# A third staging buffer for the spectrum, with a new written-out order: SSM convolution mixed with linear attention on one core

## The chip, the cores and the metric

The kernel runs on one core of one Trainium2 chip. The time is the device time of one execution in microseconds; the kernel before takes 255.44 us (median of three runs, 254.7 to 255.97). A core has TensorE (PE; its weight loads are shown as PEld), VectorE (DVE), ScalarE (ACT), GpSimd (POOL) and SyncE (SP), which here issues nearly all DMAs from one queue, in order. Each engine runs its own instructions strictly in the order in which they were written.

## The reference

Input x is [1, 2048, 512]; two branches are computed from it and mixed by a gate.

```python
x = A_u
g = sigmoid((x * gate_w).sum(-1, keepdims=True))
# branch a: a long convolution by FFT, its kernel K from a diagonal state space
dt = exp(log_dt)[:, None]
P = exp((dt * (A_re + 1j * A_im))[:, :, None] * l)          # 512 x 128 x 2048
K = einsum("dn,dnl,dn->dl", Cc, P, dt * Bc).real
a = irfft(rfft(pad(u)) * rfft(pad(K)))[:2048] + u * Dskip
# branch b: linear attention, 32 heads of 16, feature map of two softmaxes
phi(z) = concat(softmax(z @ w_phi), softmax(-(z @ w_phi)))
kv = einsum("bhsf,bhsd->bhfd", phi_k, v);  z = phi_k.sum(s)
o = (phi_q @ kv) / (phi_q @ z + 1e-6)
b = o @ wo
return g * a + (1 - g) * b
```

## The kernel before

The kernel is a graph of about 1040 nodes, each a few instructions of one engine or one DMA. Functions add nodes with their dependencies; then `Plan.run` writes them all out in one fixed order. Nothing is scheduled at run time: the string `ORDER` gives the sequence of nodes (two characters a node), `SIDES` says for each node that may run on either of two engines which one it takes (PSUM evictions, mostly, on ACT or DVE), `RINGS` says for each product that may use either of two groups of PSUM buffers which one, and `FOURS` and `ZPS` choose between two ways of doing a step. `Plan`'s first argument holds the number of buffers of each SBUF tile that rotates, among them `xst`.

In time the work runs like this.

- **Start (to about 29 us).** SP issues the loads: x transposed (`xT`, L498, in two halves of four), the value weights `WW`, the parameters of the state space, small weights, the transposed query and key weights, and x once more as `UD` in 16 DMAs (L1491). ACT makes sine tables (`TB`, `TI`, `TJ`); PE makes the first values `vp` (L678) and turns the parameters (`psri`); DVE scales them (L342 to L382); A and its high and low halves go through DRAM (`pz`, L349) into `statE` and `statC` (L358). PE folds w_phi into the weights (`wps`, L517), evicted to `WW` and `Wqp`. POOL builds index patterns, masks and `Wphi`; `selE` (L458) and `diagD` (L481) are made on DVE.
- **Keys and the spectrum of x (29 to 67 us).** For eight pairs of row blocks PE makes key products `pk`, ACT their exponentials `Ek` (both signs), PE or DVE the sums (`Zk`; `ZPS` says whether PE adds groups of four first), ACT the reciprocals (by logarithm and exponential), DVE the weighted values `vr`, and PE adds them into `kvp`. In between, the first half of the channels goes through the first FFT stages: `UDp` (copies of `UD`), PE `psA`, eviction to `XAu`, PE `psB` (L587), eviction to the staging tile `xst`, which two DMAs (L599) write to the DRAM tensor `XUd`. One `xst` tile takes two evictions (8 of 32 rows), 4 KB in each partition; there are eight such tiles, four for each half of the channels, in two buffers.
- **Tables and second half (67 to 99 us).** ACT loads the sine set; ACT and DVE in turn make the tables `Ctab` and `Dtab`. The second half of the channels goes through the same `XAu` and `xst` steps.
- **Main part (99 to 229 us).** For 16 units of 32 channels: ACT makes `E` and `cs`, DVE the factors `A` and `R` by products (L1098, L1103, L1115, L1119) and, where `FOURS` is 0, an add of two halves (L1108), PE the convolution kernel `kps` (L182; twice the matmuls where `FOURS` is 1). It is evicted (`KD`), transformed (`psA` to `XA`, `psB` to `XK`), multiplied on DVE by x's spectrum, read back from `XUd` into `XUX` (L1182, L1184), giving `t` (L1229); PE transforms back (`psz`), the result goes as `Zr` to DRAM (`Zd`, L1274) and returns turned as `ZT` (L1284); PE adds the attention output (`psy`), and DVE scales by the gate (L1362 to L1368) into `xT`. The queries (`pq`, `Eq`, `zs`, `ops`, `oT`) of four row blocks run in between; their normalisation goes through DRAM (`apd`, L897, and `ax`, L904). `ax` and `ZT` share one buffer. ACT changes between the exponential and the sine set ten times in all.
- **End (229 to 255 us).** The last 64 channels: units 12 and 13 as one group, 14 and 15 each alone (unit 15 is never written to DRAM: `pszn`, `Z`, L1353). The attention output of the fourth query block is made (`bps`, L944), scaled (`bsg`, L979 and L981, with `bs3`) and stored (L993); finished channels are stored (L1379).

`Plan` counts eight DMAs in flight (`ln`), and an issue takes one of these places.

The lines in question:

```python
X.s = g.kwk.tile([128, 4, 8, 64], BF16, name="xst", tag="xst", bufs=g.nxst)
...
P = Plan(nc, {"XAu": 1, "UDp": 1, "xst": 2, ...
g.P, g.PHASES, g.nxst = P, {0: 4, 4: 8, 8: 12, 12: 16}, P.k["xst"]
...
n.at = n.eng if isinstance(n.eng, str) else n.eng[int(next(sides, 0))]
...
for i in order:
    n = self.nodes[i]
    self.cur = n
    n.fn()
```

Of the kernel before, what the change touches and what calls it, by code (L numbers as in the profile page):

```python
# [70 lines left out]
class Plan:  # L71

    DIGITS = "0123456789abcdefghijklmnopqrstuvwxyzABCDEFGHIJKLMNOPQRSTUVWXYZ-_"
    ORDER = ("2B2C2D0H2H2K0L0K2I0E002E2L070y0d2J0j2M0I0J0M0S0N0W0P2v0T0Q0g0O010a0U0Y04050B2W0X110R0V2Q0Z0k02192w0F1612140_0h0z0G0i102T"
             "0b15171d1a0l1b2N2U0e2R2F2G4N0A2X2Y0-"
             "4L4M4O0c2O0f2x1H2V1e2S0306081w1c1f2P1n1o1p1g1q1r1s091x0m4P1y1I1z1B1Q1A1E1J0p0q0r1Y4Q1R1C2y0C0D2Z312-"
             "2_1F303334324C1D4J4K1G0n4V4X544W4Y5556571K4D4Z4-"
             "4_501S52581T0s4R1Z594E512z531U1V4F4S5a5b0t5f5h4T5c5d5e130v0w5g4U0o0u0x1O5i181N1W351P365q375s1M5j38395k3b5r5t5u5l3c3a3d3e"
             "3f5m5n5o5p5v3h3g3i5w5z5x5B5C3j3k3l3m4G5D1h1i5E5F5y5A1t3n3o5M5O1j5N5P5G3p3q3r5H3s5Q3w5I5J3x3y3z5K3t3A5R5S5L3R1L5X3D5Y5Z5-"
             "3B3E3S3T5_3U5V3F5T5U3G605W6a6c6b6d613K3L3M6e3N6f6g1X1_3u1-3V3W3X3Y3Z3-"  # L80
             "3C3_211k41203v27221l4042622363294344452b282d243H46642a2c252A4748492f2h3I2e2o3O3P4a4b1u4c2j4g4d2g2i4h262k2l2m2q4i4j664n2p"
             "2s4e4p4q4k4u2n654o2r4w4x6h6i1m3Q2t1v674v6j2u89686l8b8d4B6m8k694r4s4l8f8l888c8a6n6u8e4t3J8g6k6o6q4H8m6p4I8h8i8j4f8n8o6w6x"
             "6y6v8q8r8s6z6A6B4y8E8w4z8x8F718p8t8u4A8v7A7B4m6t6C6D6E8K7273748N6r6F6G8G8y8O7577956H8z8A8H8C768_6I8I8L787C8D6J8B797a6s7D"
             "a2a36K908J7E7F8P6L8T8U7b6M8M7c916P6Q6R8Qabac7G7H7d8R8S967e7f7g6N6Oad9U9Y9Z8V8Wa46T9V8X7h6Sa8a992936V6W9-6Ua5a6a78Y8Z8-"
             "ah9Xa06X9W6Zaiaa9_7i7j7k7la19b9c7I7Jaeaf9j7m7K7q9k7rap6Y9d7n7L7Maq7o6-"
             "7N949lagaj7O7P7Q7s7pakayaz7R7tar7Savaw977T9e9f9m9n7ubV7vbWaA9r9sbLbPasat7w7x9z7y9AbQalbM7V7W9tau7Uam7ZaEanbRao7_7z9g7X9h"
             "7-ax80aPbNaF6_98aS7YaBbS9o818370aT84aCbObTbU9982aDaG9ubX859v9a9pb_aH9B9C869DaMaN87c29wbYaUaQ9EbZc39x9yc0b-"
             "c4aIcpdMc8c99FcqaO9qaJaKaLc1cgdNdOc5chaYaZcraRc6cvcwb4a-"
             "cib5b6c7cabcdPbda_becbbkblcjezb79i9G9H9KaVb0b8dQdRcmckdScneA9Ib1bfbgaW9NdTdUcc9JaXcdeIcD9Ob2cl9Pb9dVcebmbhcfcM9L9McoeJcs"
             "cEbidWdCdGcteKdHeB9Q9R9SeFdDcudIcxcGeGeCeDcy9TbabnczcHcIdXdYcAdZcFcBcCe1dFeOcPd-"  # L90
             "d_eEe0bobpcQcRbqcXcYeHePbrb3e2cJcSdKcKe3e4bjdEbbeLeMcTe5cNbseNdJbycZbtcUcLd3e6dLdbd4dcd5eQeRc-"
             "cOe7e8cVc_bvfofpd6frddbwfqeScWd0bxenbueTfueUeVbzbAfsdebBd7dfeqd8eWfteXd1d2fvf2f3eoepbCd9dabDfRfSeYdgdhfwfxeZe-"
             "erdpbEdiesf4fUfVewf5f6djdkdldqexfXfyfWdmfzdndodseydte_f7f0etbFfTf8fYfZf-f_fAdudvg0eufBdrf1e9evg1g2g3fCfDfEeaebf9g4g6fafb"
             "fcfdbIedecfFfGg5feeeg7g8efegfffgg9dwehfhgagbgcgdfHfIfJfKfLfMgegffNfOdzekflfidAdBfmbJbKfnfjdxdyelembGbHeiejfPfQggghgjfkgi"
             "gkgl")
    SIDES = ("010100100000100011001000011000001110000000000010001011100111000000110010000000000000000000000000000000100000000000100001"
             "00001100100100000000100010001001101")
    RINGS = ("10111010000000000000000000000110000000000001000110000100000010111011111011100101011000001110000101010100000100110")
    WARM = ("000000000000000000000000000000000000000000000000000000000000000000000000000000000000000000000000000000000000000000000000"
            "000000000")  # L100
    FOURS = ("0101110101011010")
    ZPS = ("01110101")

    HOT = ("pk", "vp", "pq", "zp", "ops", "bps4", "psA", "psBu", "psB128", "psB64", "psB32", "psz", "pszn", "psyn32", "psy128", "psy64", "psy32", "kps")

# [46 lines left out]
    def run(self):  # L152
        code = {d: i for i, d in enumerate(self.DIGITS)}
        order = [64 * code[a] + code[b] for a, b in zip(self.ORDER[0::2], self.ORDER[1::2])] or list(range(len(self.nodes)))
        assert sorted(order) == list(range(len(self.nodes)))
        sides, rings, warm = iter(self.SIDES), iter(self.RINGS), iter(self.WARM)
        for n in self.nodes:
# [39 lines left out]

def prepare(P, nc, g, evict, psum):

# [431 lines left out]
def attention_keys(P, nc, g, psum, r):  # L631
# [57 lines left out]
    for s2 in range(8):  # L689
# [20 lines left out]

        def ps4(K=K, box=box, on=P.ZPS[s2] == "1"):
            if not on:
# [345 lines left out]
def plan_conv(P, nc, g, psum, r):  # L1058
# [27 lines left out]
    def kgen(units, XA, new, split=False):  # L1086
        K = Bag()
        K.done, kps, nu = [], [], len(units)
        for cc, U in enumerate(units):
            t = T[U]  # L1090
            plan_exp(P, nc, g, psum, U, t, psq, [sh])
            four = P.FOURS[U] == "1"
            c = Bag()
# [330 lines left out]
def full_kernel(tc, A_u, A_A_re, A_A_im, A_B_re, A_B_im, A_C_re, A_C_im, A_log_dt, A_Dskip,  # L1424
                B_x, B_wqkv, B_w_phi, B_wo, gate_w, out):
    nc = tc.nc
# [4 lines left out]
        return ctx.enter_context(tc.tile_pool(name=name, bufs=bufs, reuse_waits="tile", **kw))  # L1431
    with ExitStack() as ctx:
        g, fc, at = Bag(), Bag(), Bag()
        P = Plan(nc, {"XAu": 1, "UDp": 1, "xst": 2, "Ek": 2, "Zk": 2, "vr": 2, "vb": 2, "acc": 1, "r8": 3, "ax": 1, "nrm": 1, "E": 2, "cs": 4, "A": 1, "R": 2,
                      "KD": 1, "XA0": 1, "XK": 2, "Zr": 2, "XUX": 3, "ln": 8}, {"ps": 2, "p0": 2, "bk": 3, "acc": 1, "pf": 2})
        g.P, g.PHASES, g.nxst = P, {0: 4, 4: 8, 8: 12, 12: 16}, P.k["xst"]
        g.LAST = (((12, 13), True), ((14,), True), ((15,), False))
# [187 lines left out]
```

## Time and profile before

| what | value |
|---|---|
| median of three runs | 255.44 us |
| profiled execution: its own time | 256.34 us |
| profiled execution: span of the profile | 254.6 us |
| busy DVE / ACT / PE | 225.0 / 212.5 / 198.4 us |
| mean granted clock of TensorE | 0.952 |
| DMA moved | 38.03 MB, mean 149 GB/s |
| chain that ended last, shares | ACT 39%, DVE 21%, PE 15%, DMA 13%, issue 7% |

The page gives busy time by engine over the span, the span in 40 slices with the busy share in tenths, the groups of instructions by line and tile with their count and mean duration, and for each group the idle time before it with what ended it. Busy time by stretch, waits by pair, the timeline of one engine and the chain can be asked of the trace. "SPq" is SyncE's sequencer issuing a DMA: its time covers the wait before the issue only in part, and several issues of one line stand in one row with the time from the first's start to the last's end. The time of a PE row is modelled and includes the drain of its last matmul.

### The profile page before, as it was taken

To read this page: it belongs to the slowest core of one execution; us is meant where nothing else is said; L and a number is where in the kernel's file an instruction comes from. 1 tells how busy PE (TensorE), PEld (TensorE's weight loads), DVE (VectorE), ACT (ScalarE), POOL (GpSimd) and SP (SyncE) were. 2 spreads that over 40 slices of the span, in tenths; PEclk is the share of its full clock that TensorE was granted. 3 is DMA by queue.
4 is the path that set the end of the run, shared out by engine and by line. 5 is a ranking of instruction groups with operands and counts; after the bars stand their busy time and mean duration, and the time that the engine had idled before them with its cause. 6 is when DMAs were issued, how large, how long until landed. Compare 5 with 4: busy or idle time off the path is not lost.

```text
span 254.6 us, 9988 instructions
## 1 busy us (share of the span) xinstructions
PE 198.4 (78%) x4466; PEld 136.2 (53%) x4488; DVE 225.0 (88%) x308; ACT 212.5 (83%) x293; POOL 7.0 (3%) x19
## 2 busy tenths in 40 slices
PE   0295999999545769998668868998997799999940
PEld 0043466665435523565447556656775586777630
DVE  6769678897999998999999999999999999998631
ACT  4956799999899999999999999999897999744300
POOL 6040000000000000000000000000000000000000
PEclk9999999999995797999799999999999999999995
DMA  5999994009640869004340176155575397899666
GB/s 105 181 186 201 204 203 106 2 10 257 153 123 3 237 163 339 13 13 143 111 152 28 42 235 234 49 178 113 170 226 189 117 244 198 251 237 220 159 75 102
DMA packets 79755, 38.03 MB, mean 149 GB/s; under 512 B 58720, under 2 KB 74720, under 8 KB 79712
## 3 DMA queue, kind: packets, MB, share of 16 engines
q1 hardware_dynamic: 77312, 36.93, 56.3%
q8 instruction: 35, 0.57, 1.0%
q10 hardware_dynamic: 2400, 0.46, 1.0%
q14 instruction: 8, 0.07, 0.1%
HBM read 21.12 MB, written 13.11 MB: 134 GB/s over the span
## 4 chain that ended last, share of the span: by engine, by line
ACT 39%; DVE 21%; PE 15%; DMA 13%; issue 7%; SPq 4%; ACTq 0%; DVEq 0%
ACT cs L68 7%; ACT Ek L68 4%; DMA Zd<-Zr 3%; DMA XUd<-xst 3%; DMA ZT<-Zd 3%; PE kps L182 3%; ACT trg L68 3%; ACT Zr L148 3%; DVE R L1115 3%; ACT L65 3%; DVE R L1119 2%; DMA xT<-in_A_u_dram 2%; ACT XAu L148 2%; PE vp L678 2%; DVE A L1098 2%
## 5 line engine op out<-in xcount | busy, mean ns | idle before, releaser
L182 PE MATMUL kps<-R,A 128*32 128x64 bf16 x1600 | 29.6, 230 | 3.8 <-DVE A L1103 1.7
L182 PEld LDWEIGHTS <-A 128*32 128x32 bf16 x1600 | 27.6, 160 | 7.5 <-issue 2.6
L68 ACT ACTIVATE cs<-args 128x1024 bf16<-128x1024 f32 x32 | 31.1, 1082 | 0.0
L678 PE MATMUL vp<-WW,xT 128*128 128x512 bf16 x46 | 12.7, 423 | 12.6 <-DMA xT<-in_A_u_dram 11.4
L1119 DVE TENSOR_TENSOR R<-E,cs 128x2048 bf16<-128x2048 bf16 x16 | 19.5, 1219 | 0.0
L1115 DVE TENSOR_TENSOR R<-E,cs 128x2048 bf16<-128x2048 bf16 x16 | 19.5, 1219 | 0.0
L1103 DVE TENSOR_TENSOR A<-Ctab,Dtab 128x2048 bf16<-128x2048 bf16 x16 | 19.5, 1219 | 0.0
L1098 DVE TENSOR_TENSOR A<-Ctab,Dtab 128x2048 bf16<-128x2048 bf16 x16 | 19.5, 1218 | 0.0
L148 ACT CAST XK<-psB 128x1024 bf16<-128x1024 f32 (+1 forms) x17 | 16.1, 976 | 2.8 <-PE psB L195 2.6
L1229 DVE TENSOR_TENSOR t<-XUX,XK 128x2048 bf16<-128x2048 bf16 x14 | 17.0, 1219 | 1.1 <-ACT XK L148 1.1
L148 ACT CAST XA<-psA 128x1024 bf16<-128x1024 f32 (+1 forms) x16 | 15.5, 1014 | 1.8 <-PE psA L189 1.6
L68 ACT ACTIVATE Ek<-pk 128x512 bf16<-128x512 f32 x32 | 16.6, 615 | 0.4 <-PE pk L697 0.4
L68 ACT ACTIVATE Eq<-pq 128x512 bf16<-128x512 f32 (+1 forms) x28 | 16.8, 697 | 0.0
L68 ACT ACTIVATE E<-args 128x1024 bf16<-128x1024 f32 x16 | 16.8, 1060 | 0.0
L1261 PE MATMUL psz<-t,TI 128*128 128x512 bf16 x51 | 14.9, 379 | 2.2 <-DVE t L1229 0.4
L841 PE MATMUL pq<-xT,Wqp 128*128 128x512 bf16 x64 | 16.2, 386 | 0.4 <-ACT Eq L68 0.3
L148 ACT CAST Zr<-psz 128x1024 bf16<-128x1024 f32 x13 | 13.1, 1047 | 3.2 <-PE psz L1261 2.5
L587 PE MATMUL psB<-XAu,TB 64*128 64x128 bf16 x256 | 11.6, 250 | 5.1 <-ACT XAu L148 3.1
L678 PEld LDWEIGHTS <-xT 128*128 128x128 bf16 x48 | 5.0, 106 | 18.6 <-issue 14.8
L697 PE MATMUL pk<-WW,xT 128*128 128x512 bf16 x58 | 14.2, 380 | 0.6 <-issue 0.5
L587 PEld LDWEIGHTS <-TB 64*128 64x128 bf16 x256 | 9.6, 111 | 8.6 <-issue 8.4
L65 ACT ACT_TABLE_LOAD x10 | 12.8, 1283 | 0.9 <-PEq L1609 0.7
(206 smaller groups left out, 475.8 us busy)
## 6 DMA issues: line engine op xcount, KB each, us to landing
XUX<-XUd SPq DMA_DIRECT2D x32, 256.0 KB
XUd<-xst SPq DMA_DIRECT2D x8, 512.0 KB
ax<-apd SPq DMA_DIRECT2D x16, 256.0 KB
Zd<-Zr SPq DMA_DIRECT2D x15, 256.0 KB
ZT<-Zd SPq DMA_DIRECT2D x12, 256.0 KB
UD<-in_A_u_dram SPq DMA_DIRECT2D x16, 128.0 KB
XUd<-xst SPq DMA_DIRECT2D x8, 256.0 KB
out_dram<-xT SPq DMA_DIRECT2D x4, 192.0 KB
```

The source lines that it names most:

```text
L65: return self.nc.scalar.preload_act_table_set(name)
L68: return self.nc.scalar.activation(**kw)
L148: self.nc.scalar.copy(out=o, in_=i)
L182: nc.tensor.matmul(kps[32 * dj:32 * dj + 32, g4, e, :], lhsT=A[:, ka, :, :, d].rearrange("p a b -> p (a b)"), rhs=R[:, kr, d, :], start=(i ...
L587: nc.tensor.matmul(box.ps[:, c2, sl, :], lhsT=fc.TB[rows, b0:b0 + 2].rearrange("p a b -> p (a b)"), rhs=X.t[rows, k, r0 + sl].rearrange("p ...
L678: nc.tensor.matmul(box.ps[:, u, :], lhsT=xT[:, 2 * s2 + u, kt, :], rhs=g.WW[:, 4 + kt, :], start=(kt == 0), stop=(kt == 3))
L841: nc.tensor.matmul(box.ps[:, m - m0, :] if late else box.ps[:], lhsT=g.Wqp[:, kt, 128 * m:128 * m + 128], rhs=xT[:, 4 * b:4 * b + 4, kt, : ...
L1098: nc.vector.tensor_tensor(out=c.A[:, 0:2].rearrange("p o a b c -> p (o a) b c"), in0=g.C[U // 8][:, 0:2, :, d0 % 256:d0 % 256 + 32].rearra ...
L1103: nc.vector.tensor_tensor(out=c.A[:, 2:4].rearrange("p o a b c -> p (o a) b c"), in0=g.C[U // 8][:, 1:3, :, d0 % 256:d0 % 256 + 32].rearra ...
L1115: nc.vector.tensor_tensor(out=c.R[:, :, :, 32:64], in0=t.E[:, 1].unsqueeze(1).to_broadcast([128, 2, 32, 32]), in1=t.cs[:], op=ALU.mult)
L1119: nc.vector.tensor_tensor(out=c.R[:, :, :, 0:32], in0=t.E[:, 0].unsqueeze(1).to_broadcast([128, 2, 32, 32]), in1=t.cs[:, ::-1, :, ::-1], o ...
L1229: nc.vector.tensor_tensor(out=box.t, in0=Ls[r0 // ns].X[:], in1=box.XK[:].unsqueeze(1).to_broadcast([128, 2, 1024]), op=ALU.mult)
```

## The change

The staging tile `xst` gets a third buffer. The whole written order of nodes is replaced, and with it the choice of engine for the steps that have one, the choice of PSUM group, and the choices in `FOURS` and `ZPS`. The nodes, their dependencies and their instructions are the same but for these choices.

- Engines: 155 choices, of which 36 are the second kind before and 37 after. `selE` and `diagD` move from DVE to POOL. Evictions that move from DVE to ACT: two `vp`, three `XAu`, one `xst`, one `wps`, four `oT`, two `Zr`, one `Y`. From ACT to DVE: two `XAu`, two `xst`, one `wps`, two `vb`, one `XA`, one `oT`, one `bs3`, and one half each of the last `KD` and `XK`. One `bs3` and one `bsg` go to ACT, another `bsg` to DVE. Two pairs of stores of L1379 move from SP's queue to ACT's, and of the last stores two pairs change places between the queues.
- `FOURS`: the second form in units 1, 2, 3, 5, 7, 8, 9, 11, 12 after; in 1, 3, 4, 5, 7, 9, 11, 12, 14 before. `ZPS`: DVE sums alone in pairs 0, 2, 6 after; 0, 4, 6 before.
- SP's queue: two parameter loads stand before `WW` and three `xT` transposes; `wc` and the other small weights stand after the parameters; the `pz` writes of `statE`'s part stand before those of `statC`'s and after 12 of the 16 `UD` loads, the others at the end; the reads into `statE` and `statC` stand together, ahead of all `XUd` writes; the load of `wo` and the `XUX`, `ax`, `Zd` and `ZT` transfers are interleaved anew; at the end the read of the last `ZT` follows straight on the write of the last `Zd`, and the stores of L993 and the last of L1379 come behind it.
- DVE and ACT: three `Dtab` exponentials and one more `vp` eviction stand ahead of the first `Ek`; in the last unit the halves of `KD`, `XA` and `XK` are shared between both engines; the scaling `bsg` of the last query block stands behind the products of unit 15 rather than between them. On PE the two `bps` groups stand between `kps` and `psA` and between `psB` and `psz` of unit 15.

```diff
@@ class Plan
-    ORDER = ("2B2C2D0H2H2K0L0K2I0E002E2L070y0d2J0j2M0I0J0M0S0N0W0P2v0T0Q0g0O010a0U0Y04050B2W0X110R0V2Q0Z0k02192w0F1612140_0h0z0G0i102T"
...
+    ORDER = ("2H2I2J0a040H0I0E0K0J0M0S2E0b2B002F0L0N2K2L2G0d0g0P0h0i0j0k07012x0y0z0F2C2D0c0A2y190G0e2v0B2N051d2W2T0C062Q0s0f0p2U0m0T11"
...
-    SIDES = ("010100100000100011001000011000001110000000000010001011100111000000110010000000000000000000000000000000100000000000100001"
-             "00001100100100000000100010001001101")
-    RINGS = ("10111010000000000000000000000110000000000001000110000100000010111011111011100101011000001110000101010100000100110")
+    SIDES = ("111101000000000101011010011100001010000000000000000010111100001010010000000100000000000000000000000000100000000000000000"
+             "11000100010100000000100000101101110")
+    RINGS = ("11101100000000000000000000000010000000000001000111101000000000001010101101011111000101111011111100010000001001010")
...
-    FOURS = ("0101110101011010")
-    ZPS = ("01110101")
+    FOURS = ("0111010111011000")
+    ZPS = ("01011101")
@@ full_kernel
-        P = Plan(nc, {"XAu": 1, "UDp": 1, "xst": 2, "Ek": 2, "Zk": 2, "vr": 2, "vb": 2, "acc": 1, "r8": 3, "ax": 1, "nrm": 1, "E": 2, "cs": 4, "A": 1, "R": 2,
+        P = Plan(nc, {"XAu": 1, "UDp": 1, "xst": 3, "Ek": 2, "Zk": 2, "vr": 2, "vb": 2, "acc": 1, "r8": 3, "ax": 1, "nrm": 1, "E": 2, "cs": 4, "A": 1, "R": 2,
                       "KD": 1, "XA0": 1, "XK": 2, "Zr": 2, "XUX": 3, "ln": 8}, {"ps": 2, "p0": 2, "bk": 3, "acc": 1, "pf": 2})
```

## The prediction

> **What bounds the kernel now.** I read the page's sums first, then the slices, then busy time by stage, the waits, and last the SyncE queue of the final 20 us. No engine is full over the span, so the sums alone decide nothing.
>
> ```profile
> PE 198.4 (78%) x4466; PEld 136.2 (53%) x4488; DVE 225.0 (88%) x308; ACT 212.5 (83%) x293; POOL 7.0 (3%) x19
> DVE  6769678897999998999999999999999999998631
> ACT  4956799999899999999999999999897999744300
> ```
>
> The slices show VectorE (DVE) and ScalarE (ACT) both full from about 70 to 190 us, DVE alone to 229, and a thin tail. The view of busy time by stretch says it in us (length, then PE, PEld, DVE, ACT and POOL, each with its count). I cut it at ScalarE's landmarks: first exponential of the keys (28.8), second load of the sine table (67.6), second load of the exponential table (99.5), last sine load (188.9), last kernel product (229.0).
>
> ```profile
> 0.00:28.80 28.80, 13.56 (x93) 7.30 (x95) 21.45 (x52) 18.96 (x26) 7.05 (x19) 1.00 0.88 174
> 28.80:67.60 38.80, 36.47 (x725) 24.00 (x731) 32.55 (x49) 36.80 (x73) 0.00 (x0) 1.00 0.52 119
> 67.60:99.50 31.90, 20.13 (x321) 12.86 (x323) 31.24 (x54) 31.30 (x35) 0.00 (x0) 0.80 0.60 170
> 99.50:188.90 89.40, 76.99 (x1830) 52.69 (x1827) 88.67 (x100) 87.68 (x119) 0.00 (x0) 0.98 0.41 127
> 188.90:229.00 40.10, 35.61 (x949) 28.16 (x951) 38.94 (x38) 33.06 (x36) 0.00 (x0) 1.00 0.71 201
> 229.00:254.60 25.60, 15.60 (x570) 11.16 (x564) 12.14 (x18) 4.74 (x9) 0.00 (x0) 0.85 0.74 140
> ```
>
> DVE and ACT are together over 97% busy from 67.6 to 188.9; before that ACT and PE lead; after 188.9 DVE leads; in the last 25.6 us nothing is full, so a chain decides. The waits on the staging tile `xst` are small, and one long wait stands in SyncE's queue:
>
> ```profile
> DVE xst L150 <- DMA XUd<-xst: 1.7, 1, 1.7
> ACT xst L148 <- DMA XUd<-xst: 1.0, 2, 0.5
> SPq L993 <- DMA out_dram<-xT: 3.6, 1, 3.6
> ```
>
> The last is in the tail's queue, where the final read of `ZT` (L1284) stands behind the stores of L1379 and L993, and the product and scaling of the end wait for it:
>
> ```profile
> 237.27 0.35 SPq L1274 DMA_DIRECT2D Zd<-Zr  x1
> 237.67 1.00 SPq L1379 DMA_DIRECT2D out_dram<-xT  x2
> 239.50 4.29 SPq L993 DMA_DIRECT2D out_dram<-xT  x2
> 243.96 3.20 SPq L1284 DMA_DIRECT2D ZT<-Zd  x4
> 249.84 0.69 DVE L1365 TENSOR_TENSOR xT<-psy,gT 128x512 bf16<-128x512 f32 x1 [4.20 <-PE psy L1340]
> ```
>
> **The change part by part.** Durations are those of the profiled execution: span 254.6, own time 256.34; the runs' median is 255.44, so its time is 0.9 above the median. I sum differences and apply them to the median.
>
> *Work moved between engines.* Instructions overlap a little, so I count start to next start: a 1024-column eviction holds ACT 0.90 (1.01 long) and DVE 1.13 (1.22 long), a 512-column one 0.48 and 0.60, `cs` 0.95. Off DVE go `selE` (1.22) and `diagD` (0.81) to POOL, net two early `vp` evictions (2.3), two `Zr` (2.3), three of `oT` (1.8), one each of `XAu` and `Y` (1.1, 0.6). On DVE come one `xst` (1.1), two `vb` (1.2), one `XA` (1.1), and halves of the last `KD` and `XK` and one `bs3` (0.6 each). In all DVE goes from 225.6 to 219.9 (-5.7), ACT from 212.9 to 215.6 (+2.7). Ten table loads stay. FOURS has nine ones and ZPS five in both, so PE's multiplications and the adds of L1108 keep their number; of the last three units none now skips the add, where one did.
>
> Cutting the new written order at the same landmarks gives ACT/DVE work before -> after: to 28.8: 18.9/22.2 -> 21.5/18.2; to 67.6: 37.1/31.4 -> 34.4/34.2; to 99.5: 31.3/29.7 -> 32.2/31.6; to 188.9: 87.8/92.6 -> 87.0/84.8; to 229: 33.0/37.6 -> 34.8/40.4; end: 4.7/12.1 -> 5.7/10.6.
>
> *Start, to the first key exponential: 0.* ACT sat idle 9.8 of 28.8, so 2.6 more work (three `Dtab` exponentials, one eviction) fits. On SyncE two parameter loads (0.5 each) now precede the `xT` transposes, so the first `vp`, which waited to 11.43, waits about 1.1 longer; `wc` goes from 7.58 to about 11.2, and `Wphi` on POOL (waited 7.7) follows it to about 17, still ahead of `wps` at 22.57. The issues ahead of the weights' transpose add up to 14.2 against 14.39, so it and the last four `xT` transposes, which start the keys, stay put. Cover gone: +1.1. UD, pz and the statE/statC reads swap places later, read from about 90 us on: nothing, unless `UD`, ended by 36.9, ends later than the first `psA` at 43.
>
> *Keys, 28.8 to 67.6: -1.5.* ACT's work falls 2.7, but PE is busy 36.5 of 38.8 with the same products: floor -2.3. Ceiling 0, if PE's order is no better. DVE's `xst` wait of 1.7 and ACT's 0.5 here lie within these idle times; with a third buffer the fourth tile waits for the first write, not the second. Next is `Zk`, whose waits are 0.8. I take two thirds of the floor.
>
> *Tables and main part, 67.6 to 229: -1.2.* DVE 156.8 after 160.0: with its 1.4 idle, floor -3.3. The other end goes by ACT: 32.2 + 0.6 idle, then 87.0 + 1.6, then DVE's 40.4 + 0.6 give 162.4 against 161.4: +1.0. The truth is between, as both engines now carry nearly equal work; I take the middle. Queued behind waits here: `XUX` loads, `Zd` writes, apd, `ax` and the wo load share SyncE; their issue counts are equal and their longest waits (6.7 for `XUX` on `t`) are for buffers, so I count 0; a late `XUX` would stop DVE's `t` for up to the 1.2 of one `t`.
>
> *Tail, 229 to 254.6: -2.0.* In the new order the last `ZT` read stands straight behind its `Zd` write, the stores after it; two pairs of stores move to ACT's queue. `ax`, which it takes, is free when `psy` of the 64 columns ends, 240.8, so it gains at most 243.96 - 240.8 = 3.2. At least 0: stores on ACT's queue (0.87 a pair) stand ahead of `bs3` and `bsg`, and what follows waits for those. On PE the two `bps` products (1.9 each) fall into the waits for `KD` and `XK`. The last `Zr` on ACT saves 0.2. I take above half, as the 3.6 wait has a named place.
>
> The wait of 3.6 ends with a store's landing, not its issue. The Trainium skill, "DMA: Bandwidth & Descriptors", section "Issuing engines are not separate DMA queues", says that another issuing engine saves only issue time, since all share the same DMA engines. By it the moved stores would save the 1.00 of one pair and the sum be 251.7; no run here shows which.
>
> Sum: 0 - 1.5 - 1.2 - 2.0 = -4.7: 255.4 - 4.7 = **250.7**.
>
> **The rivals.** *ACT becomes the bound (slower).* ACT takes 2.7 more and keeps its idle of 42: its waits before 28.8, and its thin end, are chains. 255.4 + 2.7 = 258.1. For it: 98% in the 121 us to 188.9. Against: half its idle lies in the tail. It decides when ACT's idle falls by under 2.7. Chance 0.24.
>
> *Gains cancel.* Keys 0 because PE holds them, main part +1.0, tail -1.0 (issue time alone): 255.4. For it PE's 36.5; against, its idle in 64 to 68. Chance 0.13.
>
> *Every floor is met.* -2.3 - 3.3 - 3.2 = -8.8: 246.6. Against it: nearly equal loads leave less slack for crossings. Chance 0.12.
>
> *`selE` on POOL stops DVE.* `Wphi`, half as large, took 1.05 on POOL; `selE` would take 2.1 by that, near 18 us, where DVE's `dtc` chain runs. If that chain halts, -4.7 + 2.1: 252.8. The trace of before has no such overlap. Chance 0.05. The Trainium skill, "SBUF — State Buffer", section "Who interferes with whom", has GpSimd and two-input VectorE instructions contend for one read interface; nothing here shows it yet.
>
> **How the numbers follow.** The forecast has 0.46, the rivals 0.54. Its own range is 248.6 to 253.0, by step ends half met. For eight in ten I go from 247.0, leaving half of the floors' case, to 258.0, leaving half of ACT's. About 0.5% (1.3 us) is what a measurement here can tell from none: faster 0.46 + 0.12 + 0.05 = 0.63, same 0.13, slower 0.24.
>
> **What would show it.** In the profile after: DVE's busy sum near 220, ACT's near 215; first `Ek` at 28 to 29; second sine load near 66; no `xst` wait on a DMA; the last `kps` group starting near 226; the last `ZT` read following its `Zd` write by 3 to 4 us, and 23 to 24 us from that `kps` to the end. Wrong would be: ACT 99% full to 190 with DVE waiting for `cs` or `E` (the first rival), a first `Ek` after 30, or ACT's queue held by stores near the end.

## The result and the profile after

The changed kernel takes 255.74 us (median of 20 runs, 252.94 to 258.05), the kernel before 256.36 in the 20 runs beside it. The ratio is 0.9946, 95% interval 0.9922 to 0.9970: about 1.4 us faster (0.8 to 2.0). The ratio is taken over the runs in the faster of the two states that a kernel shows (15 of the changed kernel's 20), so it lies further from one than that of the two medians, which differ by 0.6 us. The forecast was 4.7 us.

The page of the changed kernel, its busy sums:

```profile
PE 199.7 (79%) x4467; PEld 138.5 (55%) x4488; DVE 222.2 (88%) x302; ACT 216.6 (85%) x297; POOL 11.0 (4%) x22
```

DVE lost 2.8 of busy time, where the forecast had 5.7; ACT gained 4.1, of which 1.28 is one more table load. The span is 253.4 (own time 255.21). The view by stretch (length, then PE, PEld, DVE, ACT, POOL), cut at the same landmarks as before:

```profile
0.00:29.29 29.29, 14.26 (x93) 8.44 (x95) 21.07 (x52) 22.60 (x31) 10.97 (x22) 0.94 0.89 175
29.29:65.35 36.06, 34.72 (x718) 23.20 (x723) 31.08 (x44) 34.17 (x68) 0.00 (x0) 1.00 0.56 123
65.35:98.07 32.72, 21.94 (x333) 13.56 (x336) 31.77 (x52) 32.25 (x34) 0.00 (x0) 0.84 0.51 141
98.07:186.94 88.87, 76.10 (x1858) 54.26 (x1862) 87.55 (x102) 87.25 (x120) 0.00 (x0) 0.94 0.42 129
186.94:228.91 41.97, 37.63 (x955) 28.95 (x952) 40.17 (x39) 34.57 (x38) 0.00 (x0) 1.00 0.76 216
228.91:253.40 24.49, 15.02 (x533) 10.13 (x532) 10.54 (x16) 5.80 (x10) 0.00 (x0) 0.80 0.73 135
```

Against the stretches before: start +0.5, keys -2.7 (38.80 to 36.06), tables +0.8, main part to the last sine load -0.5, from there to the last kernel product +1.9, tail -1.1. Two of these landmarks mislead, as the many profiles below showed. The second sine load stands at another place of ACT's work in the new order, so keys and tables have to be read together. The last kernel product is cut in two by a stop of PE in some profiles, so the last `R` (L1119) is the better mark for the end of the main part. Below, stages are: start (to the first `Ek`), keys and tables (to the second exponential load), main part (to the start of the last `R`), tail.

The waits of the changed kernel, by what was waited for (total, times, longest):

```profile
POOL Wphi L473 <- DMA wc<-in_B_w_phi_dram: 12.6, 1, 12.6
ACT xT L979 <- DVE xT L981: 6.4, 1, 6.4
DVE t L1229 <- ACT XK L148: 1.4, 2, 1.0
```

No tile `xst` waits for a DMA any more; `Wphi` waits 12.6 where it waited 7.7; DVE waits for ACT's `XK`, and in the tail ACT for DVE. SyncE's queue in the tail:

```profile
235.31 0.35 SPq L1274 DMA_DIRECT2D Zd<-Zr  x1
239.91 3.06 SPq L1284 DMA_DIRECT2D ZT<-Zd  x4
243.02 1.13 SPq L1379 DMA_DIRECT2D out_dram<-xT  x2
```

The last `ZT` read is issued at 239.91 after 243.96, as forecast. Yet the last scaling of DVE, which stood at 249.84, stands at 247.87: of the 4.05 that the read gained, 2.0 arrived. Both figures hold some time that was won before the tail: its first instruction, the last `R`, starts at 226.91 after 227.76. Counted from there, the read gained 3.2 and the last scaling 1.1.

### The profile page after: what moved, and what is told of

The parts are those of the page before. It is cut to its first block, busy times and chain, and to the rows that moved or that the text cites. A ratio compares the mean times of both kernels' runs of the same rounds, so it can differ in the third digit from the quotient of the medians.

```text
span 253.4 us, 9985 instructions
## 1 busy us (share of the span) xinstructions
PE 199.7 (79%) x4467; PEld 138.5 (55%) x4488; DVE 222.2 (88%) x302; ACT 216.6 (85%) x297; POOL 11.0 (4%) x22
## 4 chain that ended last, share of the span: by engine, by line
DVE 29%; ACT 28%; PE 23%; issue 9%; DMA 7%; POOL 1%; SPq 1%; ACTq 0%; DVEq 0%; POOLq 0%
DMA ZT<-Zd 5%; ACT cs L68 4%; PE pk L697 4%; DVE A L1098 3%; DVE R L1119 3%; PE kps L182 3%; PE psA L562 3%; DVE R L1115 2%; ACT Ek L68 2%; DMA Zd<-Zr 2%; DVE A L1103 2%; ACT Zr L148 2%; ACT XA L148 2%; ACT trg L68 2%; DVE E L1051 2%
## 5 line engine op out<-in xcount | busy, mean ns | idle before, releaser
L678 PE MATMUL vp<-WW,xT 128*128 128x512 bf16 x47 | 12.6, 417 | 11.7 <-DMA xT<-in_A_u_dram 11.6
L1119 DVE TENSOR_TENSOR R<-E,cs 128x2048 bf16<-128x2048 bf16 x16 | 19.5, 1217 | 0.0
L148 ACT CAST Zr<-psz 128x1024 bf16<-128x1024 f32 x15 | 15.2, 1037 | 2.3 <-PE psz L1261 2.1
L148 ACT CAST XA<-psA 128x1024 bf16<-128x1024 f32 (+1 forms) x15 | 14.6, 1009 | 1.7 <-PE psA L189 1.7
L841 PE MATMUL pq<-xT,Wqp 128*128 128x512 bf16 x64 | 15.3, 380 | 0.6 <-ACT Eq L68 0.6
L562 PE MATMUL psA<-W,UDp 128*128 128x256 bf16 x64 | 11.1, 317 | 5.2 <-ACT XAu L148 3.2
L587 PE MATMUL psB<-XAu,TB 64*128 64x128 bf16 x256 | 9.6, 225 | 4.2 <-ACT xst L148 4.2
```

The lines of the kernel that those rows point to most:

```text
L148: self.nc.scalar.copy(out=o, in_=i)
L562: nc.tensor.matmul(box.ps[:, i, :], lhsT=X.u[:, :, :, c].rearrange("p e t -> p (e t)"), rhs=fc.W1[:].rearrange("p i r d -> p (i r d)"), st ...
L678: nc.tensor.matmul(box.ps[:, u, :], lhsT=xT[:, 2 * s2 + u, kt, :], rhs=g.WW[:, 4 + kt, :], start=(kt == 0), stop=(kt == 3))
L841: nc.tensor.matmul(box.ps[:, m - m0, :] if late else box.ps[:], lhsT=g.Wqp[:, kt, 128 * m:128 * m + 128], rhs=xT[:, 4 * b:4 * b + 4, kt, : ...
L1119: nc.vector.tensor_tensor(out=c.R[:, :, :, 0:32], in0=t.E[:, 0].unsqueeze(1).to_broadcast([128, 2, 32, 32]), in1=t.cs[:, ::-1, :, ::-1], o ...
```

## The experiments

Four questions: is it the buffer or the order; did POOL cost what its rival said; what ate the tail's gain; what ate the main part's. In the first four kernels the written-out strings take four lines fewer, so their line numbers are four lower (L338 there is L342). Diffs of the order are given by the names of steps, with their lines.

### Buffer and order

The third buffer alone, on the kernel before:

```diff
-        P = Plan(nc, {"XAu": 1, "UDp": 1, "xst": 2, "Ek": 2,
+        P = Plan(nc, {"XAu": 1, "UDp": 1, "xst": 3, "Ek": 2,
```

> The kernel before with one digit changed: three staging buffers, the old order and engines. Theory A (the buffer removes the waits of DVE 1.7 and ACT 1.0 on the write of XUd, and they lay inside the keys' stretch, which PE holds): those waits are gone from the list, the second sine load comes at most 0.5 us earlier than 67.6, and the time is within 0.3% of before. Theory B (those waits were on the path): the second sine load 1 to 2 us earlier, the time 1 to 1.7 us shorter (ratio 0.993 to 0.996). By B the buffer alone is the whole gain of the change; by A the gain came with the order.

Measured: ratio 0.9952 (0.9916 to 0.9989), 254.67 us against 256.69. From the first `Ek` to the second exponential load 68.78 us after 70.73 before. Both waits on the write of `XUd` are gone from the list. The second sine load moved by only 0.4, as the start was 0.7 later in this profile; counted from the first `Ek` it came 1.1 sooner (37.68 after 38.82). Theory B by the time: the waits were on the path, and one digit gives as much as the whole change, as far as the two intervals tell. The chain that ended last in the kernel before runs through such a write twice (start, length):

```profile
56.65 4.91 DMA XUd<-xst
61.69 1.23 DVE xst L150
...
86.59 3.45 DMA XUd<-xst
90.14 1.01 ACT xst L148
```

The reverse, the changed kernel with the old two buffers:

```diff
-        P = Plan(nc, {"XAu": 1, "UDp": 1, "xst": 3, "Ek": 2,
+        P = Plan(nc, {"XAu": 1, "UDp": 1, "xst": 2, "Ek": 2,
```

> The changed kernel's order, engines and queues with the old two staging buffers; nothing else differs. The stretch from the first key exponential to the second load of the exponential table took 70.7 us before and 68.8 to 69.2 in all five kernels with a third buffer, old order or new. Theory A (the buffer is the gain and the new order is worth nothing): that stretch back to 70.5 or more, waits on the write of XUd back in the list with 2 us or more together, ratio 0.998 to 1.004. Theory B (the new order gives the same gain by another way, and the two do not add up): stretch 69.2 or less, ratio 0.993 to 0.996. Theory C (the order was made for three buffers and is bad with two): stretch over 72, ratio above 1.004.

Measured: 1.0229 (1.0195 to 1.0262), the stretch 75.47. Theory C. Its waits hold one line that no kernel with three buffers has:

```profile
ACT xst L148 <- DMA XUd<-xst: 5.3, 2, 4.8
```

ACT stands 4.8 us before an eviction whose buffer is still being written out, and all behind it in ACT's order stands too. So the new order can't do without the buffer, while the old order gains as much by it alone (0.9952) as the whole change gives (0.9946).

The new order up to the second sine load, the old one from there (three buffers):

```diff
-    ORDER = (order before)
+    ORDER = (order after, up to tabT 2) + (order before, what is left)
```

> The changed kernel's order, engines and queues up to the second sine load, and the old ones from there to the end. Theory A (the stages add up: start +0.5, keys -2.7, main +2.1, tail -1.1): second sine load near 65.3, main part back at 161 to 162, tail back at 25.5, so 2.2 us shorter than before (ratio 0.991). Theory B (what the keys give is taken back by whatever main part follows, since the same work is left over): main part 163 or more, time within 0.5% of before.

Measured: 0.997 (0.994 to 1.000). The second sine load comes at 65.33, as in the changed kernel, but the second exponential load at 98.40, 69.14 after the first `Ek`: as with the buffer alone. Theory B: what the sine load gains is given back before the next table load.

### POOL beside DVE's chain

`selE` back on DVE, in its place of the new order:

```diff
-    SIDES: selE (L458) POOL
+    SIDES: selE (L458) DVE
```

> The changed kernel with selE (L458) back on DVE in the same place of the order; nothing else differs. Theory A (selE on POOL held up two DVE instructions, the cast of L344, 1.28 long after 0.42, and the product of L345, 2.09 after 0.69, and this chain starts the keys): those two are back under 0.5 and 0.8 us, the first key exponential 0.7 to 1.5 earlier than 29.3, and the time 0.5 to 1.5 us below the changed kernel's, 0.989 to 0.993 of before. Theory B (the first key exponential waits for the last xT tiles and the weights, whose landing does not move): the first exponential within 0.3 of 29.3, time as the changed kernel's, 0.9946.

Measured: 0.9937 (0.9900 to 0.9973). POOL and DVE in the timeline of the changed kernel (start, length):

```profile
16.38 1.13 POOL L473 TENSOR_TENSOR Wphi<-wc,mask 128x512 bf16<-128x512 bf16 x1 [12.56 <-DMA wc<-in_B_w_phi_dram]
16.51 1.28 DVE L344 CAST pt<-pt 128x512 bf16<-128x512 f32 x1
17.71 0.42 DVE L344 CAST ppy<-ppy 128x512 bf16<-128x512 f32 x1
...
19.01 1.90 POOL L458 TENSOR_TENSOR selE<-m,b 128x1024 bf16<-128x1024 bf16 x1
19.37 2.09 DVE L345 TENSOR_TENSOR pt<-pt,pt 128x512 bf16<-128x512 f32 x1
```

The two casts of L344 have one shape; the one that starts while POOL runs `Wphi` takes 1.28, the other 0.42. The product of L345 beside `selE` takes 2.09; its twin took 0.69. They end 0.28 and 0.55 after POOL's instruction. With `selE` on DVE:

```profile
15.47 1.44 POOL L469 TENSOR_TENSOR Wphi<-wc,mask 128x512 bf16<-128x512 bf16 x1 [11.65 <-DMA wc<-in_B_w_phi_dram]
15.92 1.54 DVE L338 TENSOR_TENSOR ppy<-Are,dtc 128x512 f32<-128x512 bf16 x1
...
17.38 0.41 DVE L340 CAST pt<-pt 128x512 bf16<-128x512 f32 x1
...
19.42 0.92 DVE L341 TENSOR_TENSOR pt<-pt,pt 128x512 bf16<-128x512 f32 x1
```

The cast is back at 0.41, the product at 0.92 (now beside `diagD`), and `Wphi`, which came a little sooner, holds up a product of L342 instead (1.54 for 0.69). The first `Ek` comes at 28.13 after 29.29. Theory A; in the total 0.9937 cannot be told from 0.9946. The Trainium skill, "SBUF — State Buffer", section "Who interferes with whom", says that a VectorE instruction with two inputs in SBUF contends with a GpSimd instruction that reads SBUF, and that casts can take the shared ports too; these rows agree.

The rest of POOL's work taken off the chain as well, by loading `wc` sooner:

```diff
-    SP: xT par par ld par par wc gw Dcol wqk
+    SP: xT wc gw Dcol par par ld par par wqk
-    SIDES: selE (L458) POOL, diagD (L481) POOL
+    SIDES: selE (L458) DVE, diagD (L481) DVE
```

> The changed kernel with selE and diagD on DVE and the small weights' three loads (wc, gw, Dcol) moved ahead of four parameter loads on SyncE, right behind the fourth transpose of xT: POOL then works on Wphi before DVE's chain of L342 to L382 starts and on nothing large during it. With selE alone back on DVE the first key exponential came at 28.13 after 29.29, and one product of L342 was still 1.54 long after 0.69, beside Wphi. Theory A (POOL's work beside that chain is what is left to save at the start): L342, L344 and L345 at 0.7, 0.4 and 0.7 throughout, the first key exponential at 26.9 to 27.6, ratio 0.986 to 0.991. Theory B (the keys' first products wait for the weights' transpose, which is not moved): first exponential 28.0 to 28.5, ratio as with selE alone, 0.9937.

Measured: 0.9979 (0.9948 to 1.0010), first `Ek` at 28.03. All of L342 to L345 take 0.69, 0.42 and 0.69. But next in line is a landing:

```profile
22.19 1.51 PE L517 MATMUL wps<-Wphi,Dtab 128*128 128x128 bf16 x24 [0.74 <-DMA Dtab<-in_B_wqkv_dram]
```

Theory B by the profile: with POOL out of the way the chain meets the weights' transpose (`Dtab`). The time is not the 0.9937 that B gave it; the profiled execution was the fastest of this kernel's runs (253.65 for a median of 255.92).

### The tail

The old order up to the last kernel product, the new from there (three buffers):

```diff
-    ORDER = (order before)
+    ORDER = (order before, up to the last kps) + (order after, what is left)
```

> The old order, engines and queues up to the last kernel product, and the changed kernel's from there. Theory A (the tail's gain of 1.1 is the tail's own): from the last kernel product to the end 24.5 where it was 25.6, ratio 0.9955. Theory B (the moved read is followed by landings that are late by as much, and the gain came from other stages): 25.3 or more, ratio 0.998 to 1.002. Theory C (my forecast's term): 23.6, ratio 0.992.

Measured: 0.9945 (0.9917 to 0.9973). From the last kernel product to the end 25.5, where the changed kernel had 24.5 and the kernel before 25.6. The time suits A, the profile B; with the third buffer alone at 0.9952, the new tail adds nothing that these runs can show. What stands in it is seen on PE, in the changed kernel's timeline:

```profile
241.86 0.26 PE L1353 MATMUL psy<-Z,TJ 64*32 64x16 bf16 x22 [0.32 <-DVE Z L150]
243.25 0.47 PE L1353 MATMUL psy<-Z,TJ 64*32 64x16 bf16 x42 [1.13 <-issue]
...
245.33 0.59 PE L1334 MATMUL psy<-xT,ident 128*128 128x256 bf16 x2 [0.69 <-DVE xT L981]
245.85 0.31 PE L1340 MATMUL psy<-ZT,TJ 64*32 64x32 bf16 x18
247.25 0.55 PE L1340 MATMUL psy<-ZT,TJ 64*32 64x32 bf16 x46 [1.09 <-issue]
```

In the middle of two groups of 64, PE waits 1.13 and 1.09 for nothing that the profile shows ("issue"). The two stops are 128 products with their weight loads apart: 256 instructions. To see whether they belong to the work or to the count of instructions, 64 small products were put where PE idles at the start:

```diff
-            for _ in range(P.cur.warm):
-                nc.tensor.matmul(ps[:].rearrange(f"p {ax} -> p ({ax})")[:, 0:512], lhsT=ident[:], rhs=fc.TB[:, 1:9].rearrange("p a b -> p (a b)"),
+            for _ in range(64 if P.cur.i == 303 else 0):
+                nc.tensor.matmul(ps[:].rearrange(f"p {ax} -> p ({ax})")[:, 0:32], lhsT=ident[:], rhs=ident[:, 0:32],
```

> The changed kernel with 64 small products (a weight load and a product of 32 columns each, 128 instructions, result overwritten) put ahead of the first vp product, where PE sat idle for 11.6 us; nothing else differs. In the tail of the changed kernel PE stops for 1.13 us after the 22nd product of the first L1353 group and for 1.09 after the 18th of the last L1340 group, 256 instructions apart, with nothing to wait for in the profile. Theory A (these are loads of PE's code, a block of 256 instructions each, about 4.0 us from entering a block to having the next): the stops follow the count and not the work, so both come 64 products sooner: one after some 20 to 24 products of the second L1296 group of the tail, one after some 20 to 24 of the second L1353 group, 1.3 to 2.2 us each, and none inside the last L1340 group or the first L1353 group; the time within 0.4% of the changed kernel's. Theory B (the stops are waits for landings of ZT or for a semaphore that the profile does not show): they stay after the 22nd and the 18th product of the same groups.

Measured: 0.9973 (0.9947 to 0.9999). PE's tail:

```profile
240.72 0.60 PE L1296 MATMUL psz<-TI,t 128*32 128x64 bf16 x24
242.30 0.86 PE L1296 MATMUL psz<-TI,t 128*32 128x64 bf16 x40 [0.98 <-issue]
...
244.75 0.24 PE L1353 MATMUL psy<-Z,TJ 64*32 64x16 bf16 x20
246.57 0.47 PE L1353 MATMUL psy<-Z,TJ 64*32 64x16 bf16 x44 [1.58 <-issue]
246.98 0.40 PE L1334 MATMUL psy<-xT,ident 128*128 128x256 bf16 x2
247.31 0.69 PE L1340 MATMUL psy<-ZT,TJ 64*32 64x32 bf16 x64
```

Both stops moved by 64 products, into other groups, and the last group runs through. They follow the count: theory A. The first is shorter than expected (0.98 for 1.3 to 2.2).

The same by itself, ten times as many at the start:

```diff
-            for _ in range(64 if P.cur.i == 303 else 0):
+            for _ in range(640 if P.cur.i == 303 else 0):
```

> The changed kernel with 640 small products (a weight load and a product of 32 columns each: 1280 instructions, five blocks of 256) ahead of the first vp product, to measure by itself what PE needs for code that it runs through faster than it arrives. Theory A (a block takes about 4.0 us wherever it is): the 640 run with a stop at the end of every 128 of them, each stop 1 to 2.5 us, 3.6 to 4.4 us from one stop's end to the next, some 20 us in all from about 3 us on, and the kernel 8 to 12 us longer. Theory B (it is the tail's DMA traffic that makes the code late): no stops over 0.5 us, the 640 done within 13 us, the kernel at most 3 us longer.

Measured: 266.59 us, 10.9 more than the changed kernel's median. PE:

```profile
3.24 5.92 PE L1557 MATMUL vp<-ident 128*128 128x32 bf16 x223 [3.24 <-DVE one L247]
11.03 3.45 PE L1557 MATMUL vp<-ident 128*128 128x32 bf16 x128 [1.87 <-issue]
15.03 3.43 PE L1557 MATMUL vp<-ident 128*128 128x32 bf16 x128 [0.55 <-issue]
18.76 3.35 PE L1557 MATMUL vp<-ident 128*128 128x32 bf16 x128 [0.30 <-issue]
25.23 1.04 PE L1557 MATMUL vp<-ident 128*128 128x32 bf16 x33 [3.12 <-issue]
```

128 products, a stop, 128 products: from one stop's end to the next 4.00, 3.73 and 6.47 us. Theory A for the mechanism, though two of the stops are smaller than expected, since these products take 3.4 us a block and not 2.

The traces also hold the packets that bring the code: queue q8 on the page, with 16 KB in each packet.

```profile
q8 instruction: 35, 0.57, 1.1%
...
q8 instruction: 40, 0.66, 1.1%
```

The first line is the changed kernel's. The second is that of the kernel with 640 more products, or 1280 more instructions: five packets more, one for 256 instructions. Every stop of PE in the rows shown so far ends 1.3 to 1.6 us after such a packet has landed. In the tail of the changed kernel the packets run from 240.95 to 241.88 and from 244.40 to 245.69, and the stops end at 243.25 and 247.25. Where one of these stops follows another, the packet between them starts 1.1 to 1.5 after the end of the first. The one behind the 6.47 starts 3.9 after it, at 22.69, and takes no longer than the others (1.17): until then the transposes of x and the weights keep the DMA engines full (2247 packets of under 512 bytes from 20.5 to 22.5). So other DMA traffic can hold up a block, as theory B had it, though this is one case.

Whether stores do that in the tail: the changed kernel without six pairs of its late stores.

```diff
-                for c in (2 * h, 2 * h + 1):
+                for c in (2 * h, 2 * h + 1) if P.cur.i not in (864, 867, 978, 981) else ():
...
-                for c in (2 * h, 2 * h + 1):
+                for c in (2 * h, 2 * h + 1) if P.cur.i not in (913, 916) else ():
```

> The changed kernel without six pairs of its late stores (the four of L1379 and the two of L993 that are issued between 236 and 247 us); those parts of the output are not written. All else, the last ZT read and the last two pairs of stores too, is as it was. Theory A (a code block takes about 4.0 us whatever the stores do): PE still stops for 0.8 to 1.4 us after the 22nd product of the first L1353 group and after the 18th of the last L1340 group, and the last product ends within 0.5 us of where it did after the last kernel product (18.9). Theory B (the stores hold up the code, as they share the DMA engines): both stops under 0.4, the last product 1.5 to 2.2 us sooner.

Measured: 255.57 us in one run; the stops stay after the 22nd and the 18th product, 0.99 and 0.81 long, and the last product ends 18.5 us after the last kernel product (18.9). Theory A, in a single run: the stores are not what makes the code late.

If the code sets the pace, work that is made ready sooner should gain nothing. The two scalings that PE waited 0.69 for, moved into DVE's idle time:

```diff
-    DVE: Zn ou(L1368) bsg(L981) bsg(L981) ou(L1368) ou(L1365)
+    DVE: Zn bsg(L981) bsg(L981) ou(L1368) ou(L1368) ou(L1365)
```

> The changed kernel with the two scalings of L981 in the tail moved ahead of the first xT of L1368 on DVE, where it idled for 2.0 us; nothing else differs. PE's last group waited 0.66 for the second of them. Theory A (loads of PE's code set the end, about 4.0 us from entering a block to having the next): that wait of PE is gone, but the stop within the last L1340 group grows from 1.09 to 1.5 to 2.2 us, and the last product ends no sooner; ratio 0.993 to 0.997. Theory B (the stops are fixed pauses of about 1.1): the end comes 0.6 to 0.8 sooner, ratio 0.990 to 0.993.

Measured: 0.9991 (0.9948 to 1.0035). PE's last groups:

```profile
246.75 0.39 PE L1334 MATMUL psy<-xT,ident 128*128 128x256 bf16 x2
247.07 0.29 PE L1340 MATMUL psy<-ZT,TJ 64*32 64x32 bf16 x18
249.57 0.54 PE L1340 MATMUL psy<-ZT,TJ 64*32 64x32 bf16 x46 [2.21 <-issue]
```

The wait for DVE is gone, and the stop has grown from 1.09 to 2.21. From the end of the stop before (245.57) it is 4.0 us, as in the changed kernel (243.25 to 247.25). Theory A by the timeline; the ratio lies above the range that it gave, and the main part of this profile was 1.5 longer than the changed kernel's.

### The main part

New order and engines only from the second exponential load to the last kernel product (three buffers):

```diff
-    ORDER = (order before)
+    ORDER = (order before, up to tabL 2) + (order after, up to the last kps) + (order before, what is left)
```

> Three staging buffers, and the new order, engines and queues only from the second exponential load to the last kernel product; start, keys, tables and tail are as before. Theory A (the new main part costs what its wait for XK costs): from the second exponential load to the last R of L1119 128.4 to 129.3 us, where the old main part took 127.6 to 128.3; DVE waits 0.6 to 2.2 near 200 us; ratio 0.997 to 0.999, above the 0.9952 of the third buffer alone. Theory B (the main part is as long in both, and what one profile shows is scatter): 127.6 to 128.2, ratio 0.994 to 0.996. My forecast's term: 126.9, ratio 0.990.

Measured: 0.9955 (0.9920 to 0.9991); main part 128.58, with a wait of 0.99 at 200 us. The profile suits A, the time does not tell it from the buffer alone (0.9952). My forecast's term is out. DVE in the changed kernel at that place:

```profile
197.45 1.21 DVE L1119 TENSOR_TENSOR R<-E,cs 128x2048 bf16<-128x2048 bf16 x1
199.69 2.36 DVE L1229 TENSOR_TENSOR t<-XUX,XK 128x2048 bf16<-128x2048 bf16 x2 [1.03 <-ACT XK L148]
```

What makes this `XK` late stands further back in the chain that ended last: PE stops for 1.00 inside a `kps`, and ACT waits 1.57 for that `kps` before it can evict `KD` (two steps of the chain, then a row of ACT's timeline).

```profile
191.51 1.00 issue
192.51 1.04 PE kps L182 x40
...
193.57 1.01 ACT L148 CAST KD<-kps 128x1024 bf16<-128x1024 f32 x1 [1.57 <-PE kps L182]
```

The stop ends 1.6 after a packet of q8 has landed (188.73 to 190.91), so it is one for code, as in the tail. All nine profiles of the new main part have one (0.6 to 1.5 long, ACT's wait behind it 1.2 to 2.1): eight inside this `kps`, and the kernel with 64 products more in the `psA` behind it. In the old order four of five profiles have one a little later, inside a `psA` (0.6 to 0.8, ACT's wait 1.0 to 1.3). How much of the difference between the two main parts this makes is not shown.

In the old order a product `Eq` fills all but 0.50 (in the kernel before) of the time that DVE would wait for `XK`. With `Eq` put there in the new order too (and `selE` on DVE):

```diff
-    DVE: R(L1119) t(L1229) t(L1229) A(L1098) Eq(L911)
+    DVE: R(L1119) Eq(L911) t(L1229) t(L1229) A(L1098)
```

> The changed kernel with selE on DVE, and one step of DVE moved: the product Eq<-Eq,ax of L911 that followed the two t of L1229 near 200 us now stands ahead of them. In the five runs of the changed kernel's main part DVE waited there 1.03, 0.60, 1.22, 2.23 and 1.47 us for ACT's XK; in the old order, where an Eq stands in that place, it did not. Theory A (this wait is what the new order lost in the main part): no wait of DVE over 0.4 between 195 and 203 us, the stretch from the second exponential load to the last R of L1119 127.6 to 128.2 (127.9 to 129.3 with the step in its old place), ratio 0.988 to 0.992. Theory B (the wait moves to the next t, since ACT is late by its own work): a wait as long within 5 us, ratio 0.993 to 0.996.

Measured: 0.9943 (0.9909 to 0.9978), main part 128.35. The wait at 200 is gone, and DVE waits ten us on, for the next `XK`:

```profile
209.58 1.23 DVE L1229 TENSOR_TENSOR t<-XUX,XK 128x2048 bf16<-128x2048 bf16 x1 [1.10 <-ACT XK L148]
```

Theory B, though the wait moved further than I gave it. From the `KD` at 193.69 on, ACT's timeline shows no wait up to that `XK`; ahead of that `KD` it waits 1.39 for a `kps` in which PE stops for 0.91. So ACT is late by its own work on top of PE's stop, and the change had put one more `Zr` on it just there. Put back on DVE:

```diff
-    SIDES: Zr (L148, near 203 us) ACT
+    SIDES: Zr (L150, near 203 us) DVE
```

> The kernel with selE on DVE and Eq ahead of the two t, with one eviction more put back: one Zr near 203 us, which the change moved from DVE to ACT, is on DVE again, in its place of the order. With it on ACT, ACT's XK came late and DVE waited 1.10 for it at 209.6. Theory A (DVE and ACT are both full there, so what one is spared it waits for the other): that wait is under 0.4, DVE's work 1.1 more, the stretch from the second exponential load to the last R as long as without (128.4) within 0.5, ratio 0.993 to 0.996. Theory B (the Zr on ACT was a loss): the stretch 127.2 to 127.9, ratio 0.989 to 0.992.

```profile
204.83 1.22 DVE L150 CAST Zr<-psz 128x1024 bf16<-128x1024 f32 x1
...
209.50 2.35 DVE L1229 TENSOR_TENSOR t<-XUX,XK 128x2048 bf16<-128x2048 bf16 x2
```

Measured: 0.9928 (0.9892 to 0.9964), main part 128.32. The wait of 1.10 has become 1.1 of work, and the stretch is as long. Theory A: the work that DVE is spared there it waits for ACT.

Last, the stages that looked best, together: new start and keys with `selE` on DVE, old main part, new tail.

```diff
-    ORDER = (order after)
+    ORDER = (order after, up to tabL 2) + (order before, up to the last kps) + (order after, what is left)
-    SIDES: selE (L458) POOL
+    SIDES: selE (L458) DVE
```

> Three staging buffers, the changed kernel's order up to the second exponential load with selE on DVE, the old order and engines from there to the last kernel product, and the changed kernel's tail. Theory A (the stages add up: start -0.6 with selE on DVE, keys -1.5, old main part 0, new tail -0.6): from the second exponential load to the last R 127.6 to 128.3, no wait of DVE over 0.6 in it, ratio 0.988 to 0.991, below every kernel so far. Theory B (what the profiles' stages show beyond the third buffer does not add up in the time): ratio 0.993 to 0.997 as with the others.

Measured: 0.9888 (0.9835 to 0.9942), 254.45 us over six runs, the lowest median of all. Its main part took 128.65 with one wait of 0.97, longer than theory A gave it. It is faster than the kernel before; its interval overlaps that of the changed kernel, so it is not shown to beat that.

## Why the forecast was right or wrong

Profiles of the same instructions differ by 0.7 to 2.5 us in a stage, so medians over the profiles that share a stage are set side by side (us; in brackets their number and range):

| stage | old order | new order | difference | forecast |
|---|---|---|---|---|
| start, to the first `Ek` | 28.86 (4; 28.8 to 29.5) | 29.29 (6; 29.0 to 31.3) | +0.4 | 0 |
| keys and tables | two buffers 70.73 (1); three buffers 69.03 (3; 68.8 to 69.8) | 69.14 (11; 68.6 to 70.2) | -1.6 | -1.5 |
| main part, to the last `R` | 128.06 (5; 127.6 to 128.7) | 128.84 (9; 127.9 to 130.4) | +0.8 | -1.2 |
| tail, from the last `R` | 26.93 (4; 25.9 to 27.4) | 25.94 (9; 25.2 to 27.1) | -1.0 | -2.0 |

Start +0.4, keys and tables -1.6, main part +0.8 and tail -1.0 make -1.4, as the ratio gives; with ranges that overlap, it is chance that the tenths agree. The kernel before has one profile, so its 70.73 is the weakest number. The forecast's missing 3.3 are 2.0 in the main part, 1.0 in the tail and 0.4 in the start. (The forecast's keys ended at the sine load; its tables were counted with the main part.)

- **Start.** The rival of `selE` on POOL had the mechanism: `selE` took 1.90 there (2.1 by `Wphi`'s size), and DVE's product beside it took 1.40 more. The cast beside `Wphi` took another 0.86, which no term had, so it is luck that the two together, 2.3, are near 2.1. I gave that rival 0.05 because `Wphi` in the trace of before overlapped nothing. I had followed `wc`'s later load only as far as POOL meeting its deadline, not what POOL would then run beside. Of the 2.3 about 0.8 reached the first `Ek`, by the profiles with and without; behind it lies the landing of the weights' transpose.
- **Keys.** The size was right, in part by luck, as the reason was wrong. I put the gain on ACT's lighter work and counted the `xst` waits as lying within idle times, at nothing; in the old order, with the old engines, the buffer alone gives it, and the chain of the kernel before ran through the writes that were waited for. A second sine load at 66 was forecast, 65.35 came, and that said nothing: the work behind it was waiting there.
- **Main part: the step that failed.** I took DVE at 156.8 after 160.0 from a cut of the list at ACT's table loads. Work must have stood on the other side of a cut whose place had moved; which work, is not shown. Between the second exponential load and the last `R`, DVE is busy 126.4 to 126.9 in the five profiles of the old main part and 125.5 to 126.1 in the nine of the new: 0.9 less by the medians, where the list had 5.0 less behind that load (130.2 to 125.2). The sum of its gaps went from between 1.0 and 2.0 to between 2.1 and 4.8. My other bound, +1.0 by ACT, was nearer. Taking the middle of two bounds was wrong where both engines are nearly full, since work that DVE was spared came back as its wait for ACT; and PE's stop for code, behind which ACT waits, was in no term. Two sums of the forecast are off by themselves: the moves that it lists for DVE make -4.9, not -5.7 (with the 2.3 that POOL cost, near the -2.8 of the page), and the floor here is -3.2, not -3.3.
- **Tail: the step that was mis-sized.** Within the tail the read came 3.2 sooner, all of my ceiling, freed by the end of the 64-column `psy` as forecast (239.84, issue 239.91). I priced only what held the read. What stands next, PE's own code, was in no term: two stops, 2.2 us, the second where PE had before waited for `ZT` in any case. Of the 3.2, 1.1 reached the last scaling. The Trainium skill's rule of "DMA: Bandwidth & Descriptors", section "Issuing engines are not separate DMA queues", gave the tail -1.0, and -1.0 came, but not by it: the read was issued 3.2 sooner within the tail, by its new place in the queue.
- **The rivals.** ACT as the bound did not come as a loss of 2.7, and DVE is still the fuller engine, but its mechanism is what the main part shows in small. "Gains cancel", 255.4, is 1.4 off where the forecast is 3.3 off, and has two of three parts right (main part +1.0, tail -1.0); its keys at 0 are wrong, and the start's loss makes up for a quarter of that.
- **What the text asked of the profile.** DVE near 220: 222.2. ACT near 215: 216.6. First `Ek` by 29: 29.29, just outside. No `xst` wait on a DMA: right. Last `kps` near 226: 228.9, wrong. Last read 3 to 4 us behind its `Zd` write: 4.6. End 23 to 24 after that `kps`: 24.5.

Left open: the time itself does not separate the new main part from the old (0.9955 against 0.9952); its +0.8 rests on profiles. And the kernel with the third buffer, all else old but the tail, came out at 0.9945, 1.3 us above what the table's sum gives it (-1.7 and -1.0). The kernel with `wc` loaded sooner came out at 0.9979, though its first `Ek` stood 1.3 sooner than the changed kernel's.

## What to carry to other kernels

When a change comes as one small resource and a large reordering, price the resource alone first: here one digit gave as much as the whole, and the order that went with it could not do without it. Where two engines are both nearly full, count a move between them as nothing until the sum of both falls, and compare work between the same two instructions, not between landmarks that move with the order. A wait that is taken out of the end of a kernel is worth only the distance to the next one, and that may be one that no row shows yet.

## What was not expected of the hardware

- PE's code comes in blocks of 256 instructions (35 packets of 16 KB for the changed kernel, 40 with 1280 instructions more). A block took about 4.0 us to arrive, counted from the end of the last stop, in the tail (243.25 to 247.25; 245.57 to 249.57) and 3.73 to 6.47 at the start. For the two in the tail that is 1.2 or 1.3 until its packet starts, 1.3 or 1.4 for the packet, and 1.3 to 1.6 from its landing until PE goes on. 128 products of 16 to 64 columns with their weight loads ran in some 1.3 to 2.5 us, so a dense run of more than a block ends in stops of 0.7 to 2.2. The Trainium skill, "Runtime: NRT & Kernel Launch", section "Instruction fetch mechanics", gives the block of 256 instructions, which agrees, and calls the cost of crossing into the next "mostly hidden", which these stops do not bear out.
- A cast of 128x512 on DVE took 1.28 for 0.42 and a product of two inputs 2.09 for 0.69, each ending 0.28 and 0.55 after the POOL instruction beside it.
- With ACT's first copy ahead of its first table load, the changed kernel shows two table loads at the start (1.28 each, at 0.73 and 2.24) where the kernel before has one; the load before the first exponential stays at 13.57 (13.51 before), so it cost nothing there.
